# A fold's layout and a product's place in a Fourier mixing and maxout kernel

## The chip, the cores and the metric

The kernel runs on one core of a Trainium2 chip. A core has five engines that run at the same time, each through its own list of instructions in order: TensorE (PE; its weight loads are shown as PEld), VectorE (DVE), ScalarE (ACT), GpSimd (POOL) and SyncE (SP, which here only starts transfers). They wait for each other by semaphores. Data lies in SBUF, 128 partitions wide; matmuls write to PSUM, from where DVE or ACT must move results away before a buffer can be used again.

The metric is the time of the kernel on the device in microseconds (us); lower is better.

## What is computed

For each of 8 batches a 2-D Fourier transform over 3072 rows and 256 features is taken, of which the real part is kept. Then each row of 256 numbers goes through a layer: the largest of three products with 256x768 matrices, and a product with a 768x256 matrix.

```python
batch, seq, dim = (8, 3072, 256)
X = np.fft.fft(x, axis=1)
X = np.fft.fft(X, axis=2)
x = X.real.astype(np.float32).reshape(B * S, D)
h = np.maximum(np.maximum(x @ w1, x @ w2), x @ w3)
out = (h @ w_out).astype(np.float32)
```

Input and output are float32; inside, the kernel works in bfloat16 with float32 sums.

## The kernel before

The transform over 3072 rows is split into 24 x 128. A class `Mix`, one object for each batch, takes a batch through it.

**Stage one** (`Mix.s`, L327; pieces s0 to s12): a matmul for each of 64 values of `dl`. Its weights are 128 columns of `x` (four groups `g` of 24 rows), its moving operand is a 96x96 block matrix, so one matmul gives 96 numbers in each partition: 4 groups x 24 residues `r`. Four or five of them fill a PSUM tile, which ACT (in batch 0 twice DVE) copies to `ub`, in the order [dl, g, r]. A feature of the 256 is the pair (g, dl).

**Fold** (`Mix.fold`, L335): features d and 256-d are added (even part, into `zE`) and subtracted (odd part, into `zO`), which leaves 128 features of each. DVE does it in three parts, named by what they cover of `dl`: A (20 to 45), B (10 to 20 and 45 to 55), C (1 to 10 and 55 to 64 and the small rest); each with `which` 0 for even and 1 for odd. In the plan below they are called fA0, fA1, fB0, fB1, fC0, fC1. The folds of one part read `ub` forwards for one source and backwards in `dl` for the other, and one instruction covers one g. `zE` holds [128 features][24 residues], `zO` [128 features][26]: two more columns than residues, for the imaginary parts of residues 0 and 12. In the feature index, dl comes first and g last (`dl g`), and the table `dvec` (L150), from which the feature side's cosines are made, has the same order. The last copy of the odd fold is kept as `self.folded`.

**Stage two** (`Mix.k`, L356, and `Mix.end`, L383; pieces kE0 to kE2, kO0 to kO2, end): for each residue r, matmuls whose weights are the column `er[:, :, r]` or `orr[:, :, r]` of zE or zO, 128 features; neighbours lie 24 or 26 elements apart. Their moving operand is a slice of a cosine or sine table of 128 (for residues 0 and 12: 64) columns; `end` has three matmuls of one column. ACT copies each PSUM tile of 512 columns to `tE` or `tO`.

**The layer.** The feature transform and the first three matrices are multiplied into one another once, at the start (`product`, L261, `keep_product`, L273, `prep_first`, `prep_second`), into gE, gO, gD and gw. Then there are 18 units for each batch: 3 blocks (`blk`) of 512 columns x 6 slices (`jc`) of 128 hidden features. A unit (L665 to L678) is

- `unit_plus` (L392): four matmuls of 512 columns into two new PSUM tiles pse2 and pse3 (L398, L399), of which two of each exist;
- `unit_out` (L409): ACT takes the positive part of pse2 to `stmp`, DVE the larger of it and pse3, into `hp`;
- `finish` of the unit before: two matmuls that change its pse2 and pse3 to the values for the mirrored rows (L406), and `unit_out` again, into `hm`;
- ten steps of the second product of the block before (`l2_block`, L426: matmuls L422 and L446, on DVE one `ot` at L451 for each of the 12 row groups of a batch, then the stores: an indirect one from POOL, L456, and a plain one from SP, L466);
- the pieces of the next batch's transform that a written plan names for this unit.

So DVE's list runs hp, hm, ot (in two units of three), a fold where the plan has one, then the next unit's hp. A unit's pse tiles are those of two units ago, so its matmuls wait for that unit's hm. The plan (L611 to L639): from batch 1's loop on, s0 to s12 of the next batch stand in units 5 to 11, the folds in units 8 to 13 (one part of one parity each: fA0, fA1, fB0, fB1, fC0, fC1), kE0 behind fC1 in unit 13, and the rest to unit 17. In batch 0's loop, all of it starts at unit 9 and the folds stand in units 11 to 16. `turn_chunk` (L113), POOL's conversion of the loaded rows of the batch after next to bfloat16 in [dl, bb] order, four chunks a batch, waits for `folded`. `ub`, `zE` and `zO` exist once.

**The start** (L546 to L583): twelve matmuls that only warm TensorE, stage one of batch 0 with products put between its pieces, the folds of batch 0 (nothing else runs on DVE then), two further products, and k for the first 512 columns:

```python
    for k in range(13):
        m.s(k, x0f, pool=ps_s,
            evict=nc.vector.tensor_copy if k in (1, 3) else nc.scalar.copy)
        if k in (6, 9):
            early.append(product(0, len(early), 0, ps_f, "ps"))
```

Every engine's order is the order in which the program is written. Loads of x are started by SP, but for batch 0's, which POOL, SP and ACT share.

Of the kernel before, what the change touches and what calls it, by code (L numbers as in the profile page):

```python
# [10 lines left out]
BF16 = mybir.dt.bfloat16  # L11
# [22 lines left out]
def kernel(  # L34
# [9 lines left out]
    nc = tc.nc  # L44
# [17 lines left out]
    consts = ctx.enter_context(tc.tile_pool(name="consts", bufs=1))  # L62
# [2 lines left out]
    x0_pool = ctx.enter_context(tc.tile_pool(name="x0", bufs=2))  # L65
    u_pool = ctx.enter_context(tc.tile_pool(name="ubuf", bufs=1))
    z_pool = ctx.enter_context(tc.tile_pool(name="zbuf", bufs=1))
    t_pool = ctx.enter_context(tc.tile_pool(name="tbuf", bufs=2))

    m24blk = consts.tile([96, 96], BF16, tag="m24blk")  # L70
# [147 lines left out]
    for (r0, r1) in ((0, 7), (7, 13)):  # L218
# [20 lines left out]
    for fc in range(2):  # L239
# [75 lines left out]
    class Mix:  # L315

        def __init__(self, b):
            self.b = b
            self.ub = u_pool.tile([128, 64 * 96], BF16, name="ub", tag="ub")
            self.zE = z_pool.tile([128, 128 * 24], BF16, name="zE", tag="zE")  # L320
            self.tE = t_pool.tile([128, NHALF], BF16, name="tE", tag="tE")
            self.tO = t_pool.tile([128, NHALF], BF16, name="tO", tag="tO")
            self.u = self.ub.rearrange("p (dl g r) -> p dl g r", g=4, r=24)
            self.e = self.zE.rearrange("p (dl g r) -> p dl g r", g=2, r=24)
            self.o = zO.rearrange("p (dl g r) -> p dl g r", g=2, r=26)

        def s(self, k, x0, pool=ps_f, evict=nc.scalar.copy):  # L327
            (d0, d1) = DLS[k]
            ps1 = pool.tile([128, 512], FP32, name="ps1", tag="ps")
            for i in range(d1 - d0):  # L330
                nc.tensor.matmul(ps1[:, i * 96:(i + 1) * 96], x0[:, d0 + i, :], m24blk,  # L331
                                 start=True, stop=True)
            evict(out=self.ub[:, d0 * 96:d1 * 96], in_=ps1[:, 0:(d1 - d0) * 96])  # L333

        def fold(self, k, which):  # L335

            u, e, o = self.u, self.e, self.o
            dst, op = ((e, ALU.add), (o, ALU.subtract))[which]
            for (lo, hi) in (((20, 45),), ((10, 20), (45, 55)), ((1, 10), (55, 64)))[k]:
                for g in range(2):  # L340
                    nc.vector.tensor_tensor(
                        out=dst[:, lo:hi, g, 0:24], in0=u[:, lo:hi, g, :],
                        in1=u[:, 64 - lo:64 - hi:-1, 3 - g, :], op=op)
            if k < 2:
                return
            nc.vector.tensor_tensor(out=dst[:, 0, 1, 0:24], in0=u[:, 0, 1, :],
                                    in1=u[:, 0, 3, :], op=op)
            if which == 0:
                nc.vector.tensor_copy(e[:, 0, 0, :], u[:, 0, 0, :])
            else:  # L350
                nc.vector.tensor_scalar(out=o[:, 0, 0, 1:12], in0=u[:, 0, 2, 13:24],
                                        scalar1=-1.0, scalar2=None, op0=ALU.mult)
                nc.vector.tensor_copy(o[:, 0, 0, 13:24], u[:, 0, 2, 1:12])
                self.folded = nc.vector.tensor_copy(o[:, 0, 0, 24:26], u[:, 0, 2, 0:13:12])

        def k(self, which, g):  # L356

            er = self.zE.rearrange("p (c r) -> p c r", r=24)
            orr = zO.rearrange("p (c r) -> p c r", r=26)
            parts = [(r, r * 128, 128) for r in range(4 * g + 1, min(4 * g + 5, 12))]  # L360
            if g == 2:
                parts += [(0, 0, 64), (12, 12 * 128, 64)]
            ps2 = ps_f.tile([128, 512], FP32, name="ps2", tag="ps")
            c0 = 0
            for (r, k0, wd) in parts:
                outsl = ps2[:, c0:c0 + wd]
                if which == 0:
                    two = 1 <= r <= 11
                    nc.tensor.matmul(outsl, er[:, :, r], cos_t[:, k0:k0 + wd],  # L369
                                     start=True, stop=not two)  # L370
                    if two:
                        nc.tensor.matmul(outsl, er[:, :, 12 + r], sin_t[:, k0:k0 + wd],  # L372
                                         start=False, stop=True)
                else:
                    io = 24 if r == 0 else 25 if r == 12 else 12 + r
                    nc.tensor.matmul(outsl, orr[:, :, r], nsin_t[:, k0:k0 + wd],  # L376
                                     start=True, stop=False)
                    nc.tensor.matmul(outsl, orr[:, :, io], cos_t[:, k0:k0 + wd],  # L378
                                     start=False, stop=True)
                c0 += wd  # L380
            nc.scalar.copy(out=(self.tE, self.tO)[which][:, g * 512:(g + 1) * 512], in_=ps2)  # L381

        def end(self):  # L383
            er = self.zE.rearrange("p (c r) -> p c r", r=24)
            orr = zO.rearrange("p (c r) -> p c r", r=26)
            ps3 = ps_f.tile([128, 512], FP32, name="ps3", tag="ps")
            nc.tensor.matmul(ps3[:, 0:1], er[:, :, 0], cos_t[:, 64:65], start=True, stop=True)
            nc.tensor.matmul(ps3[:, 1:2], orr[:, :, 0], nsin_t[:, 64:65], start=True, stop=False)
            nc.tensor.matmul(ps3[:, 1:2], orr[:, :, 24], cos_t[:, 64:65], start=False, stop=True)
# [325 lines left out]
```

## Time and profile before

| what | value |
|---|---|
| time, median of 3 runs | 437.42 us (437.2 to 438.89) |
| the profiled execution's own time | 437.27 us |
| its span, first to last instruction | 435.5 us |
| granted TensorE clock, mean | 1.00 |
| one batch in the steady part (18 units) | 49.2 us |
| folds, L341: 128x600, 128x240, 128x216 | 473, 279, 271 ns each (zO) |
| weight loads of zE, zO / of gE, gO | 0.16 / 0.10 us each |

The profile is one execution; busy times of an engine are shares of its span, in which the durations of neighbours on one engine can overlap. A matmul's duration holds its way through the array, so its cost in a row is read from the distance between starts. A line of the group view gives the source line, the engine, the operation, what it writes and reads, the form and count, then busy us and the mean ns of one, then the idle time before it and who ended it. In a windows line stand the stretch, its length, the busy time (and instructions) of PE, PEld, DVE, ACT and POOL, the clock, the DMA engines' share and GB/s. In a timeline stand the start, the time covered, engine, line, operation and how many in a row (x).

### The profile page before, as it was taken

The numbers are of one execution on the slowest core, as the hardware profiler recorded it, in microseconds if no ns is written. First come the engines' busy times: TensorE is split into PE (matmuls) and PEld (weight loads), VectorE is DVE, ScalarE is ACT, GpSimd is POOL, SyncE is SP. The second block draws the span as 40 slices with busy tenths as digits, with TensorE's granted clock in tenths as the row PEclk, the third lists the DMA queues.
The fourth block names the chain that finished last, engine by engine and source line by source line (L and its number), as shares of the span: only waits on it lengthen the run. The fifth ranks groups of instructions, "written<-read, shape, count | busy, mean of one in ns | idle before, by whom it ended". The sixth has DMA issues, their size and how long they took to land.

```text
span 435.5 us, 9209 instructions
## 1 busy us (share of the span) xinstructions
PE 413.3 (95%) x3252; PEld 277.8 (64%) x3252; DVE 309.6 (71%) x643; ACT 274.2 (63%) x512; POOL 237.8 (55%) x256
## 2 busy tenths in 40 slices
PE   0499999999999999999999999999999999999996
PEld 0275666666676667666676667666676666665665
DVE  7766668765975688666976679666976679567673
ACT  3576668667755776657765676657765676654550
POOL 7646661796269714974279514974279612214320
PEclk9999999999999999999999999999999999999999
DMA  9999999379712968169822968159822222111313
GB/s 118 121 160 129 135 169 177 103 146 169 181 53 69 162 139 189 64 115 168 165 87 76 176 123 198 61 114 165 167 92 74 73 62 75 61 50 55 105 62 132
DMA packets 127333, 51.58 MB, mean 118 GB/s; under 512 B 109233, under 2 KB 124344, under 8 KB 127288
## 3 DMA queue, kind: packets, MB, share of 16 engines
q1 hardware_dynamic: 104936, 35.80, 44.1%
q0 software_dynamic: 20624, 14.68, 17.2%
q10 hardware_dynamic: 1728, 0.52, 0.7%
q8 instruction: 25, 0.41, 0.4%
q14 instruction: 20, 0.16, 0.2%
HBM read 28.31 MB, written 25.17 MB: 123 GB/s over the span
## 4 chain that ended last, share of the span: by engine, by line
PE 90%; DVE 3%; ACT 2%; DMA 1%; POOL 1%; SPq 1%; ACTq 0%; issue 0%; POOLq 0%
PE po L422 28%; PE pse L398 14%; PE pse L406 14%; PE pse L399 14%; PE ps L331 6%; PE po L446 4%; PE pl L438 2%; PE ps L378 1%; DMA xs<-in_x_dram 1%; PE ps L369 1%; PE ps L376 1%; PE ps L372 1%; PE warm L548 1%; POOL x L118 1%; PE psg L267 1%; SPq L100 1%
## 5 line engine op out<-in xcount | busy, mean ns | idle before, releaser
L412 ACT ACTIVATE stmp<-pse 128x512 bf16<-128x512 f32 x288 | 167.8, 604 | 57.5 <-PE pse L399 52.3
L456 POOL DMA_INDIRECT out_dram<-ot,rows_m x92 | 100.2, 1089 | 166.2 <-DVE ot L451 156.2
L413 DVE TENSOR_TENSOR hp<-pse,stmp 128x512 bf16<-128x512 f32 x144 | 99.5, 691 | 100.6 <-ACT stmp L412 61.4
L118 POOL CAST x<-xs 96x2048 bf16<-96x2048 f32 x28 | 106.2, 3801 | 10.3 <-DMA xs<-in_x_dram 7.9
L398 PE MATMUL pse<-tE,gE 128*128 128x512 bf16 x288 | 109.2, 379 | 0.4
L399 PE MATMUL pse<-tO,gO 128*128 128x512 bf16 x288 | 109.0, 379 | 0.0
L413 DVE TENSOR_TENSOR hm<-pse,stmp 128x512 bf16<-128x512 f32 x144 | 98.8, 686 | 7.6 <-ACT stmp L412 7.3
L422 PE MATMUL po<-wout_bf,hp 128*128 128x256 bf16 x576 | 86.1, 273 | 0.0
L406 PE MATMUL pse<-tO,gD 128*128 128x512 bf16 x288 | 85.6, 379 | 0.0
L422 PE MATMUL po<-wout_bf,hm 128*128 128x256 bf16 x576 | 78.6, 273 | 0.0
L333 ACT CAST ub<-ps 128x480 bf16<-128x480 f32 (+1 forms) x102 | 51.7, 556 | 35.0 <-PE ps L331 35.0
L422 PEld LDWEIGHTS <-hp 128*128 128x128 bf16 x576 | 56.4, 98 | 26.1
L422 PEld LDWEIGHTS <-hm 128*128 128x128 bf16 x576 | 56.3, 98 | 16.3
L451 DVE TENSOR_TENSOR ot<-po,even 128x512 f32<-128x512 f32 x92 | 62.8, 683 | 0.0
L406 PEld LDWEIGHTS <-gD 128*128 128x128 bf16 x288 | 27.9, 98 | 32.1
L398 PEld LDWEIGHTS <-gE 128*128 128x128 bf16 x288 | 28.6, 99 | 19.5 <-issue 0.8
L399 PEld LDWEIGHTS <-gO 128*128 128x128 bf16 x288 | 28.2, 98 | 19.9 <-issue 1.6
L446 PE MATMUL po<-gw,tO 128*128 128x512 bf16 x92 | 34.9, 379 | 0.0
L331 PE MATMUL ps<-m24blk,x 96*128 96x96 bf16 x512 | 33.3, 211 | 0.9 <-POOL x L118 0.5
L331 PEld LDWEIGHTS <-x 96*128 96x128 bf16 x512 | 30.5, 111 | 3.0 <-POOL x L118 0.7
L381 ACT CAST tO<-ps 128x512 bf16<-128x512 f32 x24 | 14.0, 585 | 24.8 <-PE ps L378 24.8
L442 ACT COPY even<-pl 128x512 f32<-128x512 f32 x46 | 27.3, 594 | 0.3
(123 smaller groups left out, 335.9 us busy)
## 6 DMA issues: line engine op xcount, KB each, us to landing
xs<-in_x_dram SPq DMA_DIRECT2D x112, 192.0 KB
out_dram<-ot SPq DMA_DIRECT2D x90, 128.0 KB
out_dram<-ot,rows_m POOLq DMA_INDIRECT x92, 3.9
w_bf<-in_moe_w_dram POOLq DMA_DIRECT2D x6, 192.0 KB, 5.9
out_dram<-ot SPq DMA_DIRECT2D x17, 64.0 KB
xs<-in_x_dram SPq DMA_DIRECT2D x8, 96.0 KB
x<-in_x_dram POOLq DMA_DIRECT2D x8, 96.0 KB, 11.3
xs<-in_x_dram ACTq DMA_DIRECT2D x4, 96.0 KB
```

The costliest lines, as they stand in the source:

```text
L118: cast = nc.gpsimd.tensor_copy(turned[b][:, :, ch * 32:(ch + 1) * 32], raw.pop((b, ch)).rearrange("p (bb dl) -> p dl bb", dl=64))
L331: nc.tensor.matmul(ps1[:, i * 96:(i + 1) * 96], x0[:, d0 + i, :], m24blk, start=True, stop=True)
L333: evict(out=self.ub[:, d0 * 96:d1 * 96], in_=ps1[:, 0:(d1 - d0) * 96])
L398: nc.tensor.matmul(pse[:, 0:n], gE[i][:, js], te, start=True, stop=False)
L399: nc.tensor.matmul(pse[:, 0:n], gO[i][:, js], to, start=False, stop=True)
L406: nc.tensor.matmul(pse, gD[i][:, js], to, start=False, stop=True, skip_group_check=True)
L412: nc.scalar.activation(out=stmp[:, 0:n], in_=pses[0][:, 0:n], func=AX.Relu)
L413: nc.vector.tensor_tensor(out=dst, in0=src3, in1=stmp[:, 0:n], op=ALU.max)
L422: nc.tensor.matmul(po, hcols(jc), wout_bf[:, jc * 256:(jc + 1) * 256], start=False, stop=(jc == NJC - 1), skip_group_check=True)
L446: nc.tensor.matmul(po, to[:, cp], gw[:, 256:768], start=True, stop=True)
L451: nc.vector.tensor_tensor(out=ot.rearrange("p (h c) -> p h c", h=2), in0=po.rearrange("p (h c) -> p h c", h=2), in1=lin.unsqueeze(1).to_br ...
L456: stored(nc.gpsimd.indirect_dma_start(out, bass.IndirectOffsetOnAxis(ap=rows_m[0:128 - lo, b * 12 + slot: b * 12 + slot + 1], axis=0), ot[ ...
```

## The change

`zE` and `zO` of batches 1 to 7 are laid out as [residue][feature], with the feature index g first, then dl. The folds write that order: their instructions run over (r, g, dl), dl innermost, with both g in one. Stage two's weights then are 128 neighbours. Batch 0 keeps [feature][residue] in buffers of its own (zE0, zO0), there with g ahead of dl as well, and its fold instructions keep their order. The sources, `ub`, stay as they are. `dvec` becomes a plain count. Two memsets for the new zO are added on POOL. In the start, the first early product is issued after s7 instead of s6 and the second after s12 instead of s9.

```diff
+    z0_pool = ctx.enter_context(tc.tile_pool(name="z0buf", bufs=1))
...
-    zO = consts.tile([128, 128 * 26], BF16, tag="zO")
+    zO = consts.tile([128, 26 * 128], BF16, tag="zO")
...
-    for g in range(2):
-        iota(dvec.rearrange("p (dl g) -> p g dl", g=2)[:, g, :], [[1, 64]], base=64 * g)
+    iota(dvec, [[1, 128]])
...
-    nc.gpsimd.memset(zO.rearrange("p (c r) -> p c r", r=26)[:, :, 24:26], 0.0)
-    nc.gpsimd.memset(zO[:, 0:26], 0.0)
+    zO0 = z0_pool.tile([128, 128 * 26], BF16, name="zO0", tag="zO0")
+    nc.gpsimd.memset(zO0.rearrange("p (c r) -> p c r", r=26)[:, :, 24:26], 0.0)
+    nc.gpsimd.memset(zO0[:, 0:26], 0.0)
+    nc.gpsimd.memset(zO[:, 24 * 128:26 * 128], 0.0)
+    nc.gpsimd.memset(zO.rearrange("p (r c) -> p r c", c=128)[:, 0:24, 0], 0.0)
...
-            self.zE = z_pool.tile([128, 128 * 24], BF16, name="zE", tag="zE")
+            if b == 0:
+                zE = z0_pool.tile([128, 128 * 24], BF16, name="zE0", tag="zE0")
+                zo, form, cut = zO0, "p (g dl r) -> p r g dl", "p (c r) -> p r c"
+            else:
+                zE = z_pool.tile([128, 24 * 128], BF16, name="zE", tag="zE")
+                zo, form, cut = zO, "p (r g dl) -> p r g dl", "p (r c) -> p r c"
+            self.e = zE.rearrange(form, g=2, dl=64)
+            self.o = zo.rearrange(form, g=2, dl=64)
+            self.er = zE.rearrange(cut, c=128)
+            self.orr = zo.rearrange(cut, c=128)
...
-            self.u = self.ub.rearrange("p (dl g r) -> p dl g r", g=4, r=24)
+            self.u = self.ub.rearrange("p (dl g r) -> p r g dl", g=4, r=24)
...
             for (lo, hi) in (((20, 45),), ((10, 20), (45, 55)), ((1, 10), (55, 64)))[k]:
+                if self.b:
+                    nc.vector.tensor_tensor(
+                        out=dst[:, 0:24, :, lo:hi], in0=u[:, :, 0:2, lo:hi],
+                        in1=u[:, :, 3:1:-1, 64 - lo:64 - hi:-1], op=op)
+                    continue
                 for g in range(2):
                     nc.vector.tensor_tensor(
-                        out=dst[:, lo:hi, g, 0:24], in0=u[:, lo:hi, g, :],
-                        in1=u[:, 64 - lo:64 - hi:-1, 3 - g, :], op=op)
+                        out=dst[:, 0:24, g, lo:hi].rearrange("p r dl -> p dl r"),
+                        in0=u[:, :, g, lo:hi].rearrange("p r dl -> p dl r"),
+                        in1=u[:, :, 3 - g, 64 - lo:64 - hi:-1].rearrange("p r dl -> p dl r"),
+                        op=op)
...
-                    nc.tensor.matmul(outsl, er[:, :, r], cos_t[:, k0:k0 + wd],
+                    nc.tensor.matmul(outsl, er[:, r, :], cos_t[:, k0:k0 + wd],
...
-                    nc.tensor.matmul(outsl, orr[:, :, r], nsin_t[:, k0:k0 + wd],
+                    nc.tensor.matmul(outsl, orr[:, r, :], nsin_t[:, k0:k0 + wd],
...
-        if k in (6, 9):
+        if k in (7, 12):
             early.append(product(0, len(early), 0, ps_f, "ps"))
```

The small copies for features 0 and 64, and `end`, are re-indexed in the same way.

More of the change, by code (lines that the diff above doesn't have):

```diff
@@ L319, in __init__ @@
             self.ub = u_pool.tile([128, 64 * 96], BF16, name="ub", tag="ub")
-            self.zE = z_pool.tile([128, 128 * 24], BF16, name="zE", tag="zE")
+            if b == 0:
[8 more added lines that the diff above has]
+            self.orr = zo.rearrange(cut, c=128)
             self.tE = t_pool.tile([128, NHALF], BF16, name="tE", tag="tE")
             self.tO = t_pool.tile([128, NHALF], BF16, name="tO", tag="tO")
-            self.u = self.ub.rearrange("p (dl g r) -> p dl g r", g=4, r=24)
-            self.e = self.zE.rearrange("p (dl g r) -> p dl g r", g=2, r=24)
-            self.o = zO.rearrange("p (dl g r) -> p dl g r", g=2, r=26)
+            self.u = self.ub.rearrange("p (dl g r) -> p r g dl", g=4, r=24)
         def s(self, k, x0, pool=ps_f, evict=nc.scalar.copy):
@@ L339, in fold @@
             for (lo, hi) in (((20, 45),), ((10, 20), (45, 55)), ((1, 10), (55, 64)))[k]:
+                if self.b:
[3 more added lines that the diff above has]
+                    continue
                 for g in range(2):
                     nc.vector.tensor_tensor(
-                        out=dst[:, lo:hi, g, 0:24], in0=u[:, lo:hi, g, :],
-                        in1=u[:, 64 - lo:64 - hi:-1, 3 - g, :], op=op)
+                        out=dst[:, 0:24, g, lo:hi].rearrange("p r dl -> p dl r"),
+                        in0=u[:, :, g, lo:hi].rearrange("p r dl -> p dl r"),
+                        in1=u[:, :, 3 - g, 64 - lo:64 - hi:-1].rearrange("p r dl -> p dl r"),
+                        op=op)
             if k < 2:
                 return
-            nc.vector.tensor_tensor(out=dst[:, 0, 1, 0:24], in0=u[:, 0, 1, :],
-                                    in1=u[:, 0, 3, :], op=op)
+            nc.vector.tensor_tensor(out=dst[:, 0:24, 1, 0], in0=u[:, :, 1, 0],
+                                    in1=u[:, :, 3, 0], op=op)
             if which == 0:
-                nc.vector.tensor_copy(e[:, 0, 0, :], u[:, 0, 0, :])
+                nc.vector.tensor_copy(e[:, :, 0, 0], u[:, :, 0, 0])
             else:
-                nc.vector.tensor_scalar(out=o[:, 0, 0, 1:12], in0=u[:, 0, 2, 13:24],
+                nc.vector.tensor_scalar(out=o[:, 1:12, 0, 0], in0=u[:, 13:24, 2, 0],
                                         scalar1=-1.0, scalar2=None, op0=ALU.mult)
-                nc.vector.tensor_copy(o[:, 0, 0, 13:24], u[:, 0, 2, 1:12])
-                self.folded = nc.vector.tensor_copy(o[:, 0, 0, 24:26], u[:, 0, 2, 0:13:12])
+                nc.vector.tensor_copy(o[:, 13:24, 0, 0], u[:, 1:12, 2, 0])
+                self.folded = nc.vector.tensor_copy(o[:, 24:26, 0, 0], u[:, 0:13:12, 2, 0])
         def k(self, which, g):
-            er = self.zE.rearrange("p (c r) -> p c r", r=24)
-            orr = zO.rearrange("p (c r) -> p c r", r=26)
+            er, orr = self.er, self.orr
             parts = [(r, r * 128, 128) for r in range(4 * g + 1, min(4 * g + 5, 12))]
@@ L368, in k @@
                     two = 1 <= r <= 11
-                    nc.tensor.matmul(outsl, er[:, :, r], cos_t[:, k0:k0 + wd],
+                    nc.tensor.matmul(outsl, er[:, r, :], cos_t[:, k0:k0 + wd],
                                      start=True, stop=not two)
                     if two:
-                        nc.tensor.matmul(outsl, er[:, :, 12 + r], sin_t[:, k0:k0 + wd],
+                        nc.tensor.matmul(outsl, er[:, 12 + r, :], sin_t[:, k0:k0 + wd],
                                          start=False, stop=True)
@@ L375, in k @@
                     io = 24 if r == 0 else 25 if r == 12 else 12 + r
-                    nc.tensor.matmul(outsl, orr[:, :, r], nsin_t[:, k0:k0 + wd],
+                    nc.tensor.matmul(outsl, orr[:, r, :], nsin_t[:, k0:k0 + wd],
                                      start=True, stop=False)
-                    nc.tensor.matmul(outsl, orr[:, :, io], cos_t[:, k0:k0 + wd],
+                    nc.tensor.matmul(outsl, orr[:, io, :], cos_t[:, k0:k0 + wd],
                                      start=False, stop=True)
@@ L383, in end @@
         def end(self):
-            er = self.zE.rearrange("p (c r) -> p c r", r=24)
-            orr = zO.rearrange("p (c r) -> p c r", r=26)
+            er, orr = self.er, self.orr
             ps3 = ps_f.tile([128, 512], FP32, name="ps3", tag="ps")
-            nc.tensor.matmul(ps3[:, 0:1], er[:, :, 0], cos_t[:, 64:65], start=True, stop=True)
-            nc.tensor.matmul(ps3[:, 1:2], orr[:, :, 0], nsin_t[:, 64:65], start=True, stop=False)
-            nc.tensor.matmul(ps3[:, 1:2], orr[:, :, 24], cos_t[:, 64:65], start=False, stop=True)
+            nc.tensor.matmul(ps3[:, 0:1], er[:, 0, :], cos_t[:, 64:65], start=True, stop=True)
+            nc.tensor.matmul(ps3[:, 1:2], orr[:, 0, :], nsin_t[:, 64:65], start=True, stop=False)
+            nc.tensor.matmul(ps3[:, 1:2], orr[:, 24, :], cos_t[:, 64:65], start=False, stop=True)
             nc.scalar.copy(out=t_mid[:, :, self.b], in_=ps3[:, 0:2])
```

## The prediction

> **What bounds the kernel now.** I read the page first: busy times, then the chain that ended last, then the fold stage of one batch, engine by engine.
>
> ```profile
> PE 413.3 (95%) x3252; PEld 277.8 (64%) x3252; DVE 309.6 (71%) x643; ACT 274.2 (63%) x512; POOL 237.8 (55%) x256
> ...
> PE 90%; DVE 3%; ACT 2%; DMA 1%; POOL 1%; SPq 1%; ACTq 0%; issue 0%; POOLq 0%
> ```
>
> TensorE sets the time: 90% of the chain is its own stream, so each ns taken out of its issue counts. DVE at 71% looks safe, but that is a mean. From batch 1 on, the six units (one unit is one pass of the `jc` loop) in which the next batch is folded look like this (windows: span, then busy PE, PEld, DVE, ACT, POOL):
>
> ```profile
> 158.30:173.80 15.50, 15.50 (x135) 10.93 (x133) 14.34 (x40) 10.31 (x20) 6.12 (x9) 1.00 0.79 173
> ```
>
> There PE is never idle and DVE is busy 14.34 of 15.50 us: the cover for slower folds is about 1.2 us a batch. The DVE timeline shows the folds (L341) between the evictions hp, hm (L413) and ot (L451):
>
> ```profile
> 160.08 0.86 DVE L341 TENSOR_TENSOR zO<-ub 128x600 bf16<-128x600 bf16 x2
> 161.09 0.69 DVE L413 TENSOR_TENSOR hp<-pse,stmp 128x512 bf16<-128x512 f32 x1
> 161.70 0.68 DVE L413 TENSOR_TENSOR hm<-pse,stmp 128x512 bf16<-128x512 f32 x1
> 162.30 0.68 DVE L451 TENSOR_TENSOR ot<-po,even 128x512 f32<-128x512 f32 x1
> 162.90 0.87 DVE L341 TENSOR_TENSOR zE<-ub 128x240 bf16<-128x240 bf16 x4
> 163.83 0.69 DVE L413 TENSOR_TENSOR hp<-pse,stmp 128x512 bf16<-128x512 f32 x1
> ```
>
> Starts of neighbours lie 0.61 us apart though each lasts 0.69: a 512-element DVE step costs 0.61 in a row, that is, its elements plus about 75 ns.
>
> **Part 1, the gain: weights with unit step.** PE timeline, starts in a row (zE is read in steps of 24 elements, x and gE in steps of one):
>
> ```profile
> 112.33 0.59 PE L331 MATMUL ps<-m24blk,x 96*128 96x96 bf16 x10
> 112.76 0.38 PE L398 MATMUL pse<-tE,gE 128*128 128x512 bf16 x1
> ...
> 126.36 0.23 PE L369 MATMUL ps<-cos_t,zE 128*128 128x128 bf16 x1
> 126.43 0.23 PE L372 MATMUL ps<-sin_t,zE 128*128 128x128 bf16 x1
> ...
> 387.05 0.17 PE L514 MATMUL psm<-t_mid,gE 128*128 128x8 bf16 x1
> 387.08 0.17 PE L516 MATMUL psm<-t_mid,gO 128*128 128x8 bf16 x1
> ```
>
> With unit-step weights, a 96-column matmul takes 43 ns ((112.76-112.33)/10) and an 8-column one 27 to 30; a 256-column one (L422) takes 109. So 128 columns should take 56 (43 + 66 x 32/160) and 64 about 37. Now those from zE take 70 (eight from 126.36 fill 0.56 us to 126.92) and those from zO 66 (eight in 0.52). Per batch: 22 x 14 + 22 x 10 + 6 of 64 columns x 30 + 3 of one column x 40 = 0.83 us. Seven batches: **-5.9 us**, all on the path. If the strided load were not what holds them, this would be 0; the 43 ns of a pair that loads as many weights speaks against that.
>
> **Part 2, the cost: the folds.** Per batch and parity, before, the starts give 0.80 us for fold A (2 x 600 elements), 0.80 for B (4 x 240), 0.75 for C (4 x 216). After, both g lie in one instruction: 1 x 1200, 2 x 480, 2 x 432. But both sources are now walked along dl, 96 elements (192 bytes) a step, where before 24 neighbours were read in a row. The groups that bound the price of one element (line, form, count; busy us, mean ns of one; idle before):
>
> ```profile
> L118 POOL CAST x<-xs 96x2048 bf16<-96x2048 f32 x28 | 106.2, 3801 | 10.3 <-DMA xs<-in_x_dram 7.9 <-PE pse L399 1.9 <-issue 0.3
> ...
> L341 DVE TENSOR_TENSOR zE<-ub 128x600 bf16<-128x600 bf16 x16 | 6.8, 466 | 0.4 <-ACT ub L333 0.4
> ...
> L30 DVE TENSOR_TENSOR w<-v,q 128x896 f32<-128x896 f32 x1 | 1.1, 1092 | 0.0
> ...
> L30 DVE TENSOR_TENSOR w<-v,q 128x768 f32<-128x768 f32 x1 | 1.0, 957 | 0.0
> ...
> L664 POOL COPY tEr<-tE 128x512 bf16<-128x512 bf16 x1 | 0.6, 613 | 0.0
> ```
>
> The fold takes 0.52 ns an element today ((466-279)/(600-240), the 240-element folds lasting 279 ns), fp32 neighbours 1.055 ((1092-957)/128). The Trainium skill (VectorE: DVE Perf Modes, "What auto-detection actually checks") gives two bf16 results a cycle only where every tensor steps by one, and these two rows agree in size; the new sources would lose it.
> Low end: 1.055 ns, if the step costs nothing more. High end: TensorE's weight loads pay at least 67/27 = 2.5 for a step, so 2.6 ns. Between lies the only elementwise row that reads SBUF in steps of 256 bytes: POOL's L118, 1.86 ns (3801/2048), against 1.2 for POOL's neighbours (L664). I take **1.9**, this nearest row, slightly up because both sources step.
> The Trainium skill (Vector Engine (DVE) Microarchitecture Reference, 5.2) measures 1.75 ns a column for two sources that hop 288 or 608 bytes and 2.50 for steps of 96 bytes; no run here shows a stepping DVE source. It is the rule against this change: by 1.75 the total below would be some 460, by 2.50 some 493, both estimates.
>
> So A costs 1200 x 1.9 + 75 = 2.36, B 2 x (912+75) = 1.97, C 2 x (821+75) = 1.79 us. Per batch DVE gets 2 x (6.12 - 2.35) = 7.5 us more, all in six units with 1.2 to spare. What is queued behind a fold is the next unit's hp, hm and ot; the first matmuls of a unit need the pse3 buffer that hm of two units ago reads (2 buffers). From plus to hp is 1.32 us (123.45 to 124.77); hp, hm take 1.22; the third matmul comes 0.43 in. Thus a unit of TensorE lasts max(its length T, lag of DVE + 2.18), and the next lag is lag + DVE work - that. Lengths of units 8 to 14, from the starts of L398, less part 1: 2.82, 2.81, 2.77, 2.60, 2.39, 2.82, 3.27. DVE work (1.22, 0.60 more where an ot falls, the fold, 0.16 and 0.42 for the small copies in fold C): 3.57, 4.17, 3.79, 3.79, 3.77, 3.43, 1.22. Lags 0, 0.75, 1.99, 1.61, 1.61, 1.59, 1.25; PE waits 0, 0.12, 1.40, 1.19, 1.40, 0.95, 0.16: **5.2 us a batch, 36.5 in seven**. The same steps with the old folds give lags below 0.4 and no wait, as the trace has it. kE0, which reads the even folds, comes about 0.3 us behind fold C; kO0 comes level with the odd ones, for 0 to 0.2 us a batch that I leave to the range; `turn_chunk` waits for `folded` (L118 behind fold C), so the casts move with the stall, and the s pieces that need them too.
>
> **Part 3, the rest.** The second product (L267, four matmuls, 0.65 us) leaves its place before s10 and stands behind s12, so fold C and kE0 of batch 0 come up to 0.65 us sooner (29.80 to about 29.2). But at 58.30 TensorE waits 0.47 us for POOL's cast of batch 1's last chunk, whose loads SP issues one per 1.3 to 1.5 us from 23.5 to 48.0 on its own; so that wait takes the gain: 0, at best -0.65. The first product behind s7 delays nothing (s8, which fold B awaits, ends at the same time). The two extra memsets (0.33 us or less) fall into POOL's idle 5.1 us before L280; without it they would hold gD, due at 35. Batch 0's folds keep order and size; one iota replaces two. The small copies write at steps of 256 bytes, 24 elements at most: under 0.1 us a batch, in the same queue. No DMA moves in any queue.
>
> **Sum.** 437.27 (span 435.5 and 1.77 around it; median 437.42, so equal) - 5.9 + 36.5 = **468**.
>
> **Rivals.**
> (a) A stepped read costs what it costs TensorE, 2.6 ns: the same steps give 9.4 us a batch, 437.3 + 66.1 - 5.9 = 497; from 2.3 ns on I count it here (485 and more). For it: zE's pairs, 70 ns at 48 bytes, against 27. Against: POOL's 1.86. The 2.50 ns that the Trainium skill measures (section 5.2, above) lies near it.
> (b) The other side: a stepped source streams at one element a cycle, 1.055 ns. Then A is 1.34, B 1.16, C 1.06; DVE gets 2.4 us more, and waits of 0.13, 0.59, 0.22 in units 11 to 13 make 0.9 a batch: 437.3 + 6.6 - 5.9 = 438. These waits hang on 0.2 to 0.6 us of lag, so 432 (none at all) to 438. It decides below some 1.1 ns; at 1.2 the same steps already give 442. For it: DVE's rows in the trace run at that rate; against: both other engines pay for steps.
> (c) 1.2 to 1.6 ns: 442 to 456, a half price that no row has.
> (d) The weights gain nothing because the pair is held by something else: +5.9, 474, inside the forecast.
>
> **Chances.** Forecast (1.6 to 2.3 ns, 456 to 485) 0.52; (a) 0.18; (c) 0.07; (b) 0.23, of which 0.14 faster, 0.07 within, 0.02 slower. A change of 0.5% is about what a measurement of this kernel tells from none. So faster 0.14, same 0.07, slower 0.79. The range, 436 to 495, leaves out (b)'s faster part and the top of (a).
>
> **What would show it.** The folds as 128x1200, 128x480, 128x432 with 2.4, 1.0, 0.9 us each (1.34, 0.65, 0.6 in (b)); LDWEIGHTS from zE and zO at 0.10 us instead of 0.16; in the fold windows DVE without idle, about 20 us long for 15.5, PE waiting for "DVE hm" before L398 or L399; the other units shorter by 0.83 us a batch; kE0 near 29.2 with s0 of batch 1 still near 58.3. The prediction falls if the folds run below 1.2 ns an element, or if PE does not wait where DVE is full.

## The result, and the profile after

The changed kernel takes 461.32 us (median of 6 runs, 460.98 to 462.38) against 437.65 us before (6 runs beside it, 437.18 to 438.89): 1.054 times the time before, with a 95% interval of 1.052 to 1.0558. The profiled execution took 461.6 us with a span of 459.8 us; the granted clock was 0.996. Code lines of the layer stand 16 further down than before (L398 is now L414, L413 is L429, L451 is L467), those of stage two 17 (L369 is L386); the folds of batches 1 to 7 are L352.

The page of the changed kernel, busy times and then the chain of work that ended last:

```profile
PE 411.7 (90%) x3196; PEld 271.3 (59%) x3252; DVE 351.2 (76%) x573; ACT 276.3 (60%) x512; POOL 266.1 (58%) x257
...
PE 60%; DVE 21%; issue 8%; ACT 5%; POOL 1%; DMA 1%; SPq 1%; ACTq 0%; DVEq 0%; POOLq 0%
```

TensorE's busy time hardly moved, so the 24 us are time in which it waits. The chain, which ran on TensorE for 90%, now runs on DVE for 21%. The busy share of DVE is a harmless-looking 76%; as before, the mean hides the stage that decides. That stage, as a windows line (span, then busy PE, PEld, DVE, ACT, POOL) over the units that hold the folds, first in the kernel before (the loop of batch 2), then in the changed one (the loop of batch 3):

```profile
156.07:172.17 16.10, 16.10 (x134) 10.80 (x133) 15.12 (x44) 11.43 (x22) 4.49 (x9) 1.00 0.80 164
```

```profile
216.40:237.30 20.90, 17.45 (x142) 11.35 (x144) 20.90 (x33) 11.76 (x22) 8.21 (x7) 1.00 0.74 144
```

DVE is now busy for all of it, TensorE for 17.45 of 20.90. From the hm with which the stretch begins to the hm behind the last odd fold lay 16.10 us before (156.07 to 172.17); now it is 21.08 (216.40 to 237.48). Groups by form of the changed kernel (busy us, mean ns of one, idle before):

```profile
L472 POOL DMA_INDIRECT out_dram<-ot,rows_m x92 | 129.8, 1411 | 163.7 <-DVE ot L467 153.4 <-issue 8.5 <-DVE hm L429 0.8
...
L414 PE MATMUL pse<-tE,gE 128*128 128x512 bf16 x280 | 106.1, 379 | 22.1 <-DVE hm L429 18.8 <-DVE hp L429 1.0 <-issue 0.3
...
L352 DVE TENSOR_TENSOR zE<-ub 128x1200 bf16<-128x1200 bf16 x7 | 15.4, 2205 | 0.0
...
L352 DVE TENSOR_TENSOR zE<-ub 128x480 bf16<-128x480 bf16 x14 | 13.0, 976 | 0.0
...
L352 DVE TENSOR_TENSOR zE<-ub 128x432 bf16<-128x432 bf16 x14 | 11.9, 892 | 0.0
...
L386 PEld LDWEIGHTS <-zE 128*128 128x128 bf16 x104 | 10.4, 105 | 1.8 <-DVE zE L367 1.5
```

The slope of the folds is (2205 - 892)/(1200 - 432) = **1.71 ns an element**; it was 0.52. The weight loads of zE take 0.105 us instead of 0.16, so the layout does for TensorE what it says. Eight matmuls with these weights start within 0.44 us:

```profile
181.00 0.22 PE L386 MATMUL ps<-cos_t,zE 128*128 128x128 bf16 x1
...
181.44 0.38 PE L414 MATMUL pse<-tE,gE 128*128 128x512 bf16 x1
```

TensorE's first matmul of the pse3 tile waits 18.8 us in all for DVE's hm. How one stall is made can be read from two timelines of the changed kernel (start, time covered), first DVE, then TensorE:

```profile
168.46 2.21 DVE L352 TENSOR_TENSOR zO<-ub 128x1200 bf16<-128x1200 bf16 x1
170.57 0.70 DVE L429 TENSOR_TENSOR hp<-pse,stmp 128x512 bf16<-128x512 f32 x1
171.17 0.70 DVE L429 TENSOR_TENSOR hm<-pse,stmp 128x512 bf16<-128x512 f32 x1
171.77 0.70 DVE L467 TENSOR_TENSOR ot<-po,even 128x512 f32<-128x512 f32 x1
172.37 1.88 DVE L352 TENSOR_TENSOR zE<-ub 128x480 bf16<-128x480 bf16 x2
174.14 0.70 DVE L429 TENSOR_TENSOR hp<-pse,stmp 128x512 bf16<-128x512 f32 x1
```

```profile
170.34 0.38 PE L414 MATMUL pse<-tE,gE 128*128 128x512 bf16 x1
170.56 0.38 PE L415 MATMUL pse<-tO,gO 128*128 128x512 bf16 x1
171.92 0.38 PE L414 MATMUL pse<-tE,gE 128*128 128x512 bf16 x1 [0.98 <-DVE hm L429]
...
175.49 0.38 PE L414 MATMUL pse<-tE,gE 128*128 128x512 bf16 x1 [0.81 <-DVE hm L429]
```

The fold holds hp and hm back until 170.57 and 171.17. TensorE issues two matmuls at 170.34 and 170.56 and needs for the third the buffer that this hm reads; hm ends at 171.87, and the third starts at 171.92. A fold of 1200 elements takes 2.11 from its start to hp's, two of 480 take 1.77.

Set side by side, the starts of equal hp in both traces stay level through units 1 to 8 of the loops of batches 3 to 6 (batch 1's loop has its pieces one unit later than these), move apart by 5.0 us from unit 8 to unit 14, come back by 1.2 in unit 15 and by 0.5 more up to the next unit 1. In these last four of the seven fold stages the gap grows from 11.2 to 24.3 us, 3.3 a batch; 24.3 is the whole difference (461.6 - 437.27). The first 11.2 hold 1.65 us that come at once in unit 6 of batch 2's loop, where no fold stands. The profile of experiment 2, which has the same layout, has no such jump, so these 1.65 us belong to this one execution and not to the change; in that profile, too, the last four stages cost 3.3 each.

### The profile page after: what moved, and what is told of

It reads as the page before. It is cut to its first block, busy times and chain, and to the rows that moved or that the text cites. A ratio compares the mean times of both kernels' runs of the same rounds, so it can differ in the third digit from the quotient of the medians.

```text
span 459.8 us, 9084 instructions
## 1 busy us (share of the span) xinstructions
PE 411.7 (90%) x3196; PEld 271.3 (59%) x3252; DVE 351.2 (76%) x573; ACT 276.3 (60%) x512; POOL 266.1 (58%) x257
## 4 chain that ended last, share of the span: by engine, by line
PE 60%; DVE 21%; issue 8%; ACT 5%; POOL 1%; DMA 1%; SPq 1%; ACTq 0%; DVEq 0%; POOLq 0%
PE po L438 18%; PE pse L422 10%; PE pse L414 10%; PE pse L415 8%; DVE hm L429 6%; DVE hp L429 4%; PE ps L341 4%; DVE zO L352 3%; PE po L462 3%; DVE zE L352 2%; DVE ot L467 2%; PE pl L454 2%; ACT stmp L428 2%; POOL x L119 1%; PE warm L564 1%
## 5 line engine op out<-in xcount | busy, mean ns | idle before, releaser
L472 POOL DMA_INDIRECT out_dram<-ot,rows_m x92 | 129.8, 1411 | 163.7 <-DVE ot L467 153.4
L429 DVE TENSOR_TENSOR hp<-pse,stmp 128x512 bf16<-128x512 f32 x144 | 99.3, 690 | 82.5 <-ACT stmp L428 44.0
L414 PE MATMUL pse<-tE,gE 128*128 128x512 bf16 x280 | 106.1, 379 | 22.1 <-DVE hm L429 18.8
L119 POOL CAST x<-xs 96x2048 bf16<-96x2048 f32 x28 | 104.6, 3745 | 8.8 <-DMA xs<-in_x_dram 6.3
L429 DVE TENSOR_TENSOR hm<-pse,stmp 128x512 bf16<-128x512 f32 x144 | 98.8, 686 | 7.7 <-ACT stmp L428 3.1
L415 PE MATMUL pse<-tO,gO 128*128 128x512 bf16 x245 | 92.7, 378 | 0.5
L467 DVE TENSOR_TENSOR ot<-po,even 128x512 f32<-128x512 f32 x92 | 62.9, 684 | 0.1
L352 DVE TENSOR_TENSOR zO<-ub 128x480 bf16<-128x480 bf16 (+2 forms) x35 | 40.4, 1190 | 0.0
L352 DVE TENSOR_TENSOR zE<-ub 128x480 bf16<-128x480 bf16 (+2 forms) x35 | 40.3, 1188 | 0.0
L414 PEld LDWEIGHTS <-gE 128*128 128x128 bf16 x288 | 28.1, 98 | 19.5 <-issue 0.7
```

The source lines that it names most:

```text
L119: cast = nc.gpsimd.tensor_copy(turned[b][:, :, ch * 32:(ch + 1) * 32], raw.pop((b, ch)).rearrange("p (bb dl) -> p dl bb", dl=64))
L352: nc.vector.tensor_tensor(out=dst[:, 0:24, :, lo:hi], in0=u[:, :, 0:2, lo:hi], in1=u[:, :, 3:1:-1, 64 - lo:64 - hi:-1], op=op)
L414: nc.tensor.matmul(pse[:, 0:n], gE[i][:, js], te, start=True, stop=False)
L415: nc.tensor.matmul(pse[:, 0:n], gO[i][:, js], to, start=False, stop=True)
L429: nc.vector.tensor_tensor(out=dst, in0=src3, in1=stmp[:, 0:n], op=ALU.max)
L467: nc.vector.tensor_tensor(out=ot.rearrange("p (h c) -> p h c", h=2), in0=po.rearrange("p (h c) -> p h c", h=2), in1=lin.unsqueeze(1).to_br ...
```

## The experiments

All times are medians; "before" is the kernel before, run beside them on the same chip: 437.63 us for the first four, 437.82 for the next four, 437.32 for the last four. The products stand at their new places (k in 7 and 12) in the first alone and at the old ones (6 and 9) in all others. The first and the third start from the kernel before, the others from the changed one.

**1 and 2: the two halves of the change.** First the products' move alone, in the kernel before; then the layout alone.

```diff
-        if k in (6, 9):
+        if k in (7, 12):
```

> The kernel before with only the two early products moved (behind s7 and s12). Theory: TensorE's wait at 58.3 us for batch 1's rows swallows what the start gains, so 437.6, within 0.3 of the kernel before; kE0 of batch 0 up to 0.6 us sooner, the first s0 of batch 1 where it was. Rival: the start is on the path and the move is worth its 0.65 us: 437.0 or a little less.

Measured: 437.55 us, ratio 1.0004 [0.9981, 1.0028]. TensorE's timeline in the loop of batch 0, where the next batch's first piece begins:

```profile
59.26 0.60 PE L331 MATMUL ps<-m24blk,x 96*128 96x96 bf16 x10 [1.73 <-POOL x L118]
```

kE0 of batch 0 begins at 29.54 us, 0.26 sooner than before (29.80), so the move does what it says. But TensorE then waits 1.73 us for POOL's cast, where it waited 0.47, and this piece starts no sooner than before: 59.26 against 58.30, as the loads came later in this execution (the cast of the last chunk starts at 55.51, before at 54.51).

> The changed kernel with the products back in their old places. Theory: all of the loss belongs to the folds' layout, so 461.3, as the whole change. Rival: the product's new place costs something by itself (its profile shows a start 0.5 us later): 460.8 or less.

Measured: 461.38 us, ratio 1.0551 [1.0534, 1.0567]. The move is worth nothing that can be measured; the layout is the whole loss.

**3 and 4: the two halves of the layout.** The third reads the old zE and zO, in batches 1 to 7, as if they lay [residue][feature]; the fourth has the new folds and reads the weights in steps. Both so compute other numbers than the reference.

```diff
+            if self.b:
+                er = self.zE.rearrange("p (r c) -> p c r", c=128)
+                orr = zO.rearrange("p (r c) -> p c r", c=128)
```

> The kernel before, folds and layout unchanged, but in batches 1 to 7 stage two takes its weights as 128 neighbours of zE and zO (other numbers than the residue's). Theory: the gain of part 1 stands alone on TensorE's stream: 431.5 to 432 (5.9 us less), pairs 56 ns apart, PE never waiting in the fold windows. Rival: something else holds the pairs 67 to 70 ns apart: 437.6.

Measured: 433.06 us (431.07 to 434.12), ratio 0.9909 [0.989, 0.9928]: -4.6 us, and -6.2 in the profiled run (431.07 against 437.27 of the profile before). TensorE has this gain to itself when DVE has time.

```diff
-            self.er = zE.rearrange(cut, c=128)
-            self.orr = zo.rearrange(cut, c=128)
+            self.er = zE.rearrange("p (c r) -> p r c", c=128)
+            self.orr = zo.rearrange("p (c r) -> p r c", c=128)
```

> The changed kernel's folds and layout, but stage two's weights in batches 1 to 7 taken at steps of 24 or 26 elements as before (other numbers than the residue's); products in their old places. Theory: the stepped folds cost what the changed kernel lost plus what its weights gained, 461.3 + 5.9 = 467; 465 to 467 if some of the gain fell into TensorE's waits. Rival: the loss comes from elsewhere (other buffers, stage two) and this is well below 461.

Measured: 464.68 us, ratio 1.0632 [1.0613, 1.065]. The folds alone cost 27.0 us, the whole change 23.7 (both in this group of runs), so beside slow folds the weights are worth 3.3. That lies inside the interval of the 4.6 (3.2 to 4.8), so the medians do not show that the two halves act on each other. The starts of equal hp, taken against the kernel before, say the same: in a steady batch the weights alone gain 0.78 us, the folds alone lose 4.0, and both together lose 3.3. The parts add up to within 0.1 us a batch.

**5: the step on the output instead.** The new layout, but the fold walks the 24 residues innermost: both sources are neighbours, and the output moves by 256 bytes an element.

```diff
-                if self.b:
+                if False:
```

> Layout as in the changed kernel, products in their old places, but the folds of all batches walk r innermost and each g by itself: sources are read as 24 neighbours, and the output is written at steps of 128 elements (256 bytes). Theory (a step costs DVE on whichever side it lies, about 1.7 ns an element): 600 elements 1.1 to 1.2 us, the same loss, 460 to 466. Rival (only stepped reads are dear; a stepped write leaves one element a cycle, 1.055 ns): 600 elements 0.78 us, and by the sum of the prediction 438 or, with twice the instructions, 440.

Measured: 572.89 us, ratio 1.3074 [1.2996, 1.3151]. Both expectations missed. Groups by form of one fold stage (150 to 200 us):

```profile
L357 DVE TENSOR_TENSOR zE<-ub 128x600 bf16<-128x600 bf16 x2 | 5.5, 2943 | 0.0
...
L357 DVE TENSOR_TENSOR zE<-ub 128x216 bf16<-128x216 bf16 x4 | 4.0, 1298 | 0.0
```

(2943 - 1298)/384 = 4.28 ns an element: an output stepped by 256 bytes is far dearer here than two sources stepped by 192. TensorE then waited 74.2 us for hm at the same matmul as in the changed kernel, and its granted clock fell to a mean of 0.919, which lengthens its own work too (L414 took 401 ns in the mean instead of 379).

**6: the same shapes without the step.** Everything as in the changed kernel, but the folds read the same stretches of ub as neighbours (so other numbers come out).

```diff
+                    (s0, s1) = (self.ub[:, c0 * 96:(c0 + hi - lo) * 96].rearrange(
+                        "p (r g dl) -> p r g dl", g=4, r=24) for c0 in (lo, 65 - hi))
...
-                        out=dst[:, 0:24, :, lo:hi], in0=u[:, :, 0:2, lo:hi],
-                        in1=u[:, :, 3:1:-1, 64 - lo:64 - hi:-1], op=op)
+                        out=dst[:, 0:24, :, lo:hi], in0=s0[:, :, 0:2, :],
+                        in1=s1[:, :, 3:1:-1, ::-1], op=op)
```

> The changed kernel's folds with the same shapes and outputs, but in batches 1 to 7 both sources are read as neighbours inside the same stretch of ub (other numbers than the reference's); products in their old places. Theory: the step is the cost, so without it 1200 elements take 0.7 us (two a cycle) or 1.40 us (one a cycle, 1.055 ns), TensorE's waits fall to 0 to 0.9 us a batch, 431.5 to 438. Rival: the fused form over r, g and short rows of dl is itself slow: 1200 elements still above 1.8 us and 455 or more.

Measured: 431.73 us, ratio 0.9852 [0.9794, 0.9911]. Groups by form:

```profile
L354 DVE TENSOR_TENSOR zE<-ub 128x480 bf16<-128x480 bf16 x14 | 6.6, 515 | 0.0
...
L354 DVE TENSOR_TENSOR zE<-ub 128x432 bf16<-128x432 bf16 x14 | 5.8, 496 | 0.0
L354 DVE TENSOR_TENSOR zE<-ub 128x1200 bf16<-128x1200 bf16 x7 | 5.6, 803 | 0.0
```

The same instructions on neighbours cost (803 - 496)/768 = 0.40 ns an element. The step of the sources, and not their larger size or the order of the output, is the whole loss: 461.38 - 431.73 = 29.7 us. What remains, -6.1 us (3.9 to 9.0 by the ratio's interval), is the gain of the weights without a stall: a steady batch is 0.78 us shorter, as in experiment 3.

**7: ACT turns the data.** ub lies [r][g][dl], ACT's eviction writes that order, with r innermost, in steps of 512 bytes (the 128 bytes of the expectation are the step of g), and the folds read neighbours.

```diff
+                evict(out=self.u[:, :, :, d0:d1].rearrange("p r g dl -> p dl g r"),
+                      in_=ps1[:, 0:(d1 - d0) * 96].rearrange("p (dl g r) -> p dl g r", g=4, r=24))
```

> The whole computation: in batches 1 to 7 ACT writes ub in the order [r][g][dl] (its output stepped by 128 bytes), so that the folds read and write neighbours; products in their old places. If ACT pays nothing for the step: folds as in the run with unit sources, 432 to 438, better than both kernels at its low end. If ACT pays about 0.8 ns an element more (480 elements 0.95 us for 0.56): two evictions, two stmp and part of an even copy are 3.3 us in units of 2.8, and TensorE waits for ps buffers instead: 445 or more.

Measured: 547.84 us, ratio 1.2488 [1.2416, 1.2561]. The eviction, in the groups by form:

```profile
L345 ACT CAST ub<-ps 128x480 bf16<-128x480 f32 x84 | 189.5, 2494 | 7.2 <-PE ps L342 6.8 <-issue 0.4
```

2494 ns where it took 562: 4.0 ns more an element. ACT pays for a stepped output as DVE does.

**8: the cost spread out.** If the stall comes from DVE being full in six units, folds cut in twelve, one in each of units 5 to 16, should be hidden by the idle time of those units. For batches 4 to 7; batches 1 to 3 keep the old layout. To make room, stage one starts at unit 3, and POOL's casts wait for fold A only.

```diff
+    spread = (("s0", "s1"), ("s2", "s3", "s4"), ("fA0a", "s5"), ("fA0b", "s6"), ("fA1a", "s7"),
+              ("fA1b", "s8"), ("fB0a", "s9"), ("fB0b", "s10"), ("fB1a", "s11"), ("fB1b", "s12"),
+              ("fC0a",), ("fC0b",), ("fC1a", "kE0"), ("fC1b",), ("kO0",),
+              ("kE1",), ("kO1",), ("kE2",), ("kO2", "end"))
...
+                if (k, which, part) == (0, 1, 1):
+                    self.folded = last
```

> The whole computation: batches 4 to 7 in the new layout, batches 1 to 3 in the old one; for batches 4 to 7 the folds are cut into twelve instructions of about 1 us, one a unit in units 5 to 16, stage one begins at unit 3, and the casts of the next rows wait for fold A only. Theory (the loss is lack of DVE time in six units, not DVE's total): each unit now has about 1 us of DVE time to spare, TensorE waits little, and the weights' gain of 0.83 us in each of four batches is left: 434 to 436. Rival (stepped folds slow other work, or the later stage two is on the path): 440 or more.

Measured: 480.99 us, ratio 1.0968 [1.09, 1.1037], a plain miss. The timeline of all engines, folds and casts only:

```profile
210.97 0.96 DVE L354 TENSOR_TENSOR zE<-ub 128x480 bf16<-128x480 bf16 x1
...
212.81 3.71 POOL L120 CAST x<-xs 96x2048 bf16<-96x2048 f32 x1
...
213.65 3.71 DVE L354 TENSOR_TENSOR zE<-ub 128x480 bf16<-128x480 bf16 x1
```

```profile
218.26 3.67 POOL L120 CAST x<-xs 96x2048 bf16<-96x2048 f32 x1
...
218.48 4.30 DVE L354 TENSOR_TENSOR zO<-ub 128x480 bf16<-128x480 bf16 x1
```

A fold of 480 elements takes 0.96 us by itself. The two that meet a cast end at 217.36 and 222.78, the casts at 216.52 and 221.93: 0.84 and 0.85 us before. So the fold does not share with the cast; it waits for the cast's end and then runs. A third fold, whose record starts at 224.50, 0.17 before that of its cast, waits for it in the same way (ends 229.18 and 228.34), so the starts of the records do not tell which of the two comes first. An ot, with one operand in PSUM, takes its usual 0.67 us under the first of these casts (213.05). The Trainium skill (SBUF — State Buffer, "SBUF: two separate sides") describes such a lock: a DVE operation with two sources in SBUF and a POOL operation that reads SBUF exclude each other for a whole instruction. The two ends above agree with it. In the loop of batch 6, which has spread folds and no casts, hp falls no further behind the kernel before (45.4 us in unit 6, 42.9 in unit 16). The wait for `folded` is what keeps casts and folds apart; this experiment had shortened it.

**9: ACT reads in steps, and writes short runs.** ub lies [g][r][dl]; ACT reads PSUM in steps of 96 numbers and writes runs of four or five. The folds read neighbours along dl. It computes all that the reference does.

```diff
+            self.u = self.ub.rearrange("p (g r dl) -> p r g dl" if b else "p (dl g r) -> p r g dl",
+                                       g=4, r=24)
+            self.u96 = self.ub.rearrange("p (c dl) -> p c dl", dl=64)
...
+                evict(out=self.u96[:, :, d0:d1],
+                      in_=ps1[:, 0:(d1 - d0) * 96].rearrange("p (dl c) -> p c dl", c=96))
```

> The whole computation: in batches 1 to 7 ub is laid out as [g][r][dl]; ACT reads PSUM at steps of 96 float32 and writes runs of 4 or 5 neighbours, so no output is stepped one element at a time; the folds read neighbours; products in their old places. If a stepped write is what cost ACT 4 ns an element in the last call and a stepped read of PSUM costs little: evictions of 480 below 0.9 us, 431 to 436, better than both kernels. If the read or the short runs cost ACT as much as half of that (1.5 us an eviction): 450 or more.

Measured: **434.92 us** (6 runs, 433.43 to 436.35), ratio 0.9942 [0.9919, 0.9966]: below both kernels. Groups by form:

```profile
L346 ACT CAST ub<-ps 128x480 bf16<-128x480 f32 x84 | 53.3, 694 | 25.9 <-PE ps L343 25.4
...
L358 DVE TENSOR_TENSOR zE<-ub 128x1200 bf16<-128x1200 bf16 x7 | 5.8, 828 | 0.0
```

The eviction takes 0.69 us instead of 0.56, the folds are as cheap as in experiment 6. But of that experiment's 6.1 us only 2.4 are there: a steady batch gains 0.36 us where the weights give 0.78. In the trace the units with stage one lose about 0.06 us each, most of it in unit 6 (0.15), where ten matmuls take 0.58 us (206.89 to 207.47) in place of 0.43. Why is not settled.

**10: TensorE turns the data.** As 9, but the matmul writes PSUM in steps of 20 bytes, and ACT reads neighbours.

```diff
+            turned = ps1[:, 0:(d1 - d0) * 96].rearrange("p (c dl) -> p c dl", c=96)
...
+                nc.tensor.matmul(turned[:, :, i] if self.b else ps1[:, i * 96:(i + 1) * 96],
```

> The whole computation: as the run before this one, but the turn is made by TensorE: each stage-one matmul of batches 1 to 7 writes its 96 columns at steps of 5 (or 4) float32 in PSUM, and ACT reads PSUM in order and writes runs of 4 or 5. If TensorE writes steps of 20 bytes at its own pace and ACT writes short runs freely: pairs 43 ns apart, evictions 0.56 us, 431 to 433. If the stepped PSUM write costs TensorE 1 ns a column: 64 x 0.1 us a batch, 45 us, 475 or more.

Measured: 449.30 us, ratio 1.0274 [1.0256, 1.0291], which neither expectation had. Ten matmuls of 96 columns take 0.78 us (208.27 to 209.05) instead of 0.43, and 448 of them by 35 ns more make 15.7 us. Less some 5.5 for the weights (seven times 0.78), that is 10.2 of the 12.0 us lost. ACT's eviction:

```profile
L347 ACT CAST ub<-ps 128x480 bf16<-128x480 f32 x84 | 53.2, 692 | 41.6 <-PE ps L344 41.6
```

692 ns here with neighbours read, 694 with steps of 96 numbers in experiment 9: the stepped read of PSUM costs ACT nothing, the short runs written cost it 0.13 us.

**11: half the cost.** Even folds as in the changed kernel, odd ones reading neighbours (so other numbers come out). If DVE's lateness is a queue with some cover, half of the extra work costs much less than half of the time.

```diff
+                if self.b and which:
+                    (s0, s1) = (self.ub[:, c0 * 96:(c0 + hi - lo) * 96].rearrange(
+                        "p (r g dl) -> p r g dl", g=4, r=24) for c0 in (lo, 65 - hi))
```

> The changed kernel's shapes with the even folds stepped as in the change and the odd folds reading neighbours inside the same stretch of ub (other numbers); products in their old places. Theory (a queue: DVE's extra time first uses up the 1.2 us of idle time and some 1.3 us of lag that a batch can bear, and only the rest is TensorE's wait): with 1.71 ns for the stepped parity the unit sums give 1.5 us of wait a batch, 442 to 443. Rival (each stepped fold slows TensorE in proportion): half way between 431.7 and 461.4, 446.5.

Measured: 440.23 us, ratio 1.0067 [1.0048, 1.0086]. Against 431.73 with no stepped fold (from 437.82 before) and 461.38 with all, half costs 9.0 us ((440.23 - 437.32) - (431.73 - 437.82)) of 29.7, a third. That fits a queue and not a loss in proportion, and the cover is somewhat larger than the working had it (442 to 443): a steady batch is 0.39 us longer than before, which with 0.78 for the weights makes 1.2 us of waits where the working had 1.5.

**12: experiment 8 without the casts.** POOL's casts for batches 5 to 7 are left out, so these work on older data.

```diff
-                at(b, folds + (0, 1, 3, 5)[ch], lambda b=b, ch=ch: turn_chunk(
-                    b + 2, ch, mix(b + 1).folded))
+                if b + 2 <= OLD:
+                    at(b, folds + (0, 1, 3, 5)[ch], lambda b=b, ch=ch: turn_chunk(
+                        b + 2, ch, mix(b + 1).folded))
```

> The spread kernel of the last call without POOL's casts of the rows of batches 5 to 7 (these batches compute with batch 4's rows), so that nothing of POOL but the scattered stores lies beside the stepped folds; folds and plan unchanged. Theory: the spread failed because stepped folds that overlap a cast took 3.7 to 4.7 us instead of 0.96; without casts they take 0.88 to 1.2 us each, the twelve fit into the units' idle DVE time, and the time is 433 to 436. Rival: the later stage two or the early stage one of the spread plan is what costs: 455 or more.

Measured: 440.31 us, ratio 1.006 [1.0039, 1.0081]. By source line (shortest, median and longest of the folds in ns):

```profile
L354 DVE TENSOR_TENSOR zE<-ub x24: 878/980/1208, 199.9 to 373.2; 128x600 bf16<-128x600 bf16 x8, 128x480 bf16<-128x480 bf16 x8, 128x432 bf16<-128x432 bf16 x8
```

No fold is above 1.21 us any more, and 40.2 of experiment 8's 43.2 us are gone. So nearly all of its loss was the meeting with the casts. With them out of the way, TensorE is not idle in units 5 to 16 of the loops of batches 5 and 6. The result still misses the 433 to 436 expected: a batch is 0.8 us longer than before where the weights alone make it 0.8 shorter. Of these 1.6 us, 1.05 are TensorE's idle time in units 3 and 4 (0.62 before 293.28, 0.43 before 297.11), where pieces of stage one stand on top of late pieces of stage two and wait for ACT to empty their PSUM tiles; the rest is not explained. A spread plan that also keeps casts and folds apart was not tried.

## Why the prediction held, point by point

- **The sign and the place: right.** TensorE waits for hm at the third matmul of a unit, DVE has no idle time in the fold units, and the units with stage two are shorter. Experiments 2, 4 and 6 show the cause: the step of the folds' sources.
- **The price of an element: 1.71, not 1.9 ns.** This is the term that was mis-sized. The row it came from, POOL's cast at 1.86, was the nearest in the trace, but of another engine, and the slight rise for two stepped sources was wrong. Fold A took 2.12 (217.00 to 219.12) for a predicted 2.36 us, B 1.78 for 1.97, C 1.61 for 1.79. With 1.71 the same unit sums give 4.1 us a batch in place of 5.2, and 437.3 + 28.7 - 5.9 = 460.1; the profiled run took 461.6. The step from DVE's extra work to TensorE's waits thus held: experiment 4, the folds alone, loses 4.0 us a steady batch, and the 3.3 of the whole change is that less the gain of the weights. The Trainium skill (Vector Engine (DVE) Microarchitecture Reference, section 5.2) has 1.75 ns for two hopping sources; the estimate by it, 460, was nearer than the forecast. Its 2.50 was for steps half as long as these, and did not apply.
- **The waits, unit by unit: right, but for one ot.** The working counts an ot in unit 12 that stands in unit 13 in both traces (169.83 before, 234.36 after). At its place, and with 1.71, the waits of units 10 to 14 become 1.07, 1.01, 1.22, 0.19 and 0.60, again 4.1 in all, so the slip cost the forecast nothing. Each shows at the third matmul of the unit that follows: in batch 4's loop these come late by 1.15, 0.97, 1.19 and 0.15 us (276.85, 280.42, 283.99, 286.96), and in place of the last TensorE is late by 0.47 at kO0 (289.38).
- **The weights: right in size.** Pairs in the changed kernel lie 55 to 56 ns apart, as predicted (eight from 181.00 fill 0.44 us). A steady batch gains 0.78 us by them in experiments 3 and 6, for a predicted 0.83. Over the whole time they bring 4.6 us alone (interval 3.2 to 4.8 from the ratio's 0.989 and 0.9928) and 6.1 in experiment 6 (3.9 to 9.0), for a predicted 5.9. Rival (d) is out.
- **The products' move: 0, as taken.** In the changed kernel's own profile kE0 does not come sooner (30.27 for a predicted 29.2), since stage one began 0.36 later in that execution (21.36 against 21.00) and the first product took 320 ns a matmul instead of 163. Experiment 1 shows both halves of the reason: kE0 sooner, though by 0.26 and not 0.6, and the wait for POOL's cast behind it.
- **The other rivals.** (b) fell with the first fold row, 1.71 against 1.055, and (a) with it; (c) needed 1.6 at most.
- **A wait left to the range:** kO0 waits for the odd folds as foreseen, 7 times, 4.0 us in seven batches; 0.57 a batch by the weight loads' waits; in the one at 184.45 TensorE itself is idle for 0.32. The 0 to 0.2 left to the range was low, but this wait stands where the sums have the last wait for hm, so it does not come on top of the 4.1.

## What to carry to other kernels

A layout that frees one engine's reads is paid by whoever writes it: price the producer's step on the producer's engine and in the units where that work stands, not against the engine's mean busy share. Where a transposition must be made somewhere, look for an access that takes a step for nothing (here ACT's read of PSUM) and keep runs of a few neighbours on the written side. And before work is moved in time, find out what every wait in the old order kept apart.

## What the runs showed of the hardware

- A step on a bf16 output costs much more than on the sources: 4.28 ns an element on DVE at 256 bytes (experiment 5) and 4.0 more on ACT at 512 bytes (experiment 7), against 1.71 for two sources at 192 bytes and 0.40 for neighbours on DVE. The steps are not of one length; no run has an output and a source at the same step.
- A two-source fold and a POOL cast exclude each other (experiment 8). POOL's indirect stores are drawn in as well: L472 took 1411 ns in the mean against 1089 before and 1134 with unstepped folds. Most stores take 0.96 to 0.98 us in either kernel. Before, 7 of 92 took more than 2 us, one a batch and none beside a fold; in the changed kernel 26 do. The other 19 all start while a stepped fold runs and end 0.8 to 1.2 us after it (2.69 us from 221.28, the fold from 220.91 to 223.13).
- A matmul that writes PSUM in steps of 20 bytes takes 78 ns for 96 columns instead of 43 (experiment 10).
- With TensorE busy for 79% of the span its mean granted clock was 0.919 (experiment 5), with 83% 0.934 (experiment 7), with 88% 0.972 (experiment 8); in the changed kernel, busy for 90%, it stayed at 0.996.
